# The order of a pair's seven products, and the steps of the work beside them, in an adaptive-norm block with linear attention and a Mish layer

## The chip, the cores and the metric

The kernel runs on one core of one Trainium2 chip. Its metric is the device time of one execution in microseconds, the median of several. A core has five engines with a queue of instructions each: TensorE (PE in the profile, its weight loads PEld), VectorE (DVE), ScalarE (ACT), GpSimd (POOL) and SyncE (SP, which here only starts DMAs).

## The reference

One sequence of 2048 tokens of width 512 goes through a block with two halves. Every product is in float32.

```
mod = silu(c) @ w_mod                       # six rows of 512: sa, ca, ga, sb, cb, gb
h = layernorm(x) * (1 + ca) + sa
x = x + ga * linear_attention(h) @ wo       # 32 heads of 16
h = layernorm(x) * (1 + cb) + sb
x = x + gb * (mish(h @ w1 + b1) @ w2)       # w1: 512 x 1792, w2: 1792 x 512
```

The change lies in the last line alone, in the product `h @ w1` with its Mish.

## The kernel before

**Tiles.** The tokens are worked on in four blocks of 512. The hidden width of 1792 is 14 columns of 128, and these go in 7 **pairs** (`g`). A tile is 128 partitions by 512. A float32 product is made of three products of halves: each operand is split into a high and a low half (`split`, L71: the high half by ScalarE at L75, the low half by VectorE at L80), and `mm3` or `product` multiplies high by high, low by high and high by low.

**Seven products for eight.** For two token blocks and two columns at once, the first layer is a 2 by 2 matrix product, and the kernel makes it with seven block products in place of eight (a scheme after Strassen and Winograd). A product (`product`, L911 to L919) is six matmuls of 128x512 at L917 into one PSUM bank. `pair_unit` (L933) issues the seven products of a pair:

- `a11*b11` by `pair_begin` (L924): written into a bank, the accumulator **p11**, and copied out by ScalarE as `u1` (L927),
- `s2*t2`, `s3*t3`, `s1*t1` and `a22*t4`, which VectorE adds up one after the other (`add`, L922: `u2`, `u3`, `c22`, again `u3`),
- `a12*b21`, which is added onto p11 (`pair_first`, L930), so that p11 is **written twice**, with ScalarE's copy between the writings,
- `s4*b22`, which is added onto the bank of `s1*t1`; VectorE then makes `c12` of it.

Four Mish evaluations follow on ScalarE: of `c22` and `c12` at once by `mish_b` (L909, for the other token block), and of p11 and the last `u3` by `mish` (L886, with its split, for this token block). That of p11 reads the PSUM bank itself.

**Banks.** PSUM has eight banks of one tile each, in three groups (`PBUFS`, L36): "acc" has 4, "h" has 3, "tp" has 1. A new tile of a group waits until the readers of the bank that it takes over are done. p11 takes the "tp" bank (in one pair of the last blocks an "acc" bank), the other products "h" banks.

**Order.** The order of the work is written out by hand: every engine gets its instructions in the order in which the program issues them, and works them in that order. Work beside the products is written as generators: `spawn` adds one to a list, and `tick` (L53) lets each generator on the list issue its next step. `pair_unit` has three ticks, and one tick follows every step of the second layer (`d_unit`, L891, in `trail`, L1003). On the list are, among others: `rows` (L575), which makes the operands of a later pair from w1 (four small sums on VectorE at L586 to L589, then splits); `w2_job` (L507), which scales two rows of w2 (L513), splits them and stores them; and `norm_tile` (L751), which normalizes one tile of 128 tokens for the blocks 2 and 3 in three steps: two sums on ScalarE (L210, L211); a small VectorE step (L215) and a power on GpSimd (L189); a small VectorE step (L219), the normalization on ScalarE (L198) and a store on GpSimd's DMA queue. Eight such tiles are taken from the list `tiles` in `trail`.

**Where the pairs stand.** For token blocks 0 and 1 there are seven pairs, from about 204 us on, with steps of the second layer of block 0 between them (twelve matmuls each; one step after each of the first two pairs, two steps later on). Pairs 0 and 1 have had both writings of p11 done ahead of the loop, so inside `pair_unit` p11 is written in pairs 2 to 6. Then follows the second layer of block 1 (`second`, L960). For blocks 2 and 3 ("the last blocks", `L` in the code) there are seven pairs in the order 5, 6, 0, 1, 2, 3, 4, from 357 us on; after all but the first of these `e_unit` (L1057) issues 24 narrow matmuls of the second layer, which is done by seven products as well, with `left_trail` (L1075) preparing its operands. From about 442 us on only the second layer is left.

Of the kernel before, what the change touches and what calls it, by code (L numbers as in the profile page):

```python
# [25 lines left out]
def block_kernel(ctx: ExitStack, tc: tile.TileContext, x, wqkv, wo, w1, b1t, w2, c, wmodt, out):  # L26
# [11 lines left out]
    def sb(name, dt=F32, shape=(P, 512)):  # L38

        return big.tile(list(shape), dt, tag="T", name=name, bufs=SLOTS)  # L40

    def ps(tag, name, shape=(P, 512)):
        return psp.tile(list(shape), F32, tag=tag, name=name, bufs=PBUFS[tag])
# [6 lines left out]
    def spawn(gen):  # L50
        fresh.append(gen)

    def tick():  # L53

        running.extend(fresh)
        fresh.clear()
        for g in list(running):
            if next(g, "end") == "end":
                running.remove(g)

    def run(gen):
        for _ in gen:
            pass
# [7 lines left out]
    def split(name, t, keep, key, lo_engine=dve, hi_engine=act):  # L71

        hi, lo = sb(f"{name}h", F32R, t.shape), sb(f"{name}l", F32R, t.shape)
        if hi_engine is act:
            act.activation(hi, t, AF.Copy)  # L75
        else:
            hi_engine.tensor_copy(hi, t)
        if lo_engine is dve:
            yield
        lo_engine.tensor_tensor(lo, t, f32(hi), op=ALU.subtract)  # L80
        keep[key] = hi, lo
# [18 lines left out]
    c0 = sb("c0")  # L100
# [474 lines left out]
    def rows(g, wait):  # L575

        r = [sb(f"w1p_{g}_{i}", F32, (P, 4, P)) for i in range(2)]
        for i in range(2):
            f = 2 * g + i
            sp.dma_start(r[i], w1[:, P * f:P * (f + 1)].rearrange("(k p) f -> p k f", p=P))  # L580
        for _ in range(wait):
            yield
        a11, a12, a21, a22 = [r[i][:, 2 * k:2 * k + 2, :] for i in range(2) for k in range(2)]
        s12, s34 = [sb(f"s{n}_{g}", F32, (P, 4, P)) for n in (12, 34)]
        s1, s2, s3, s4 = s12[:, 0:2, :], s12[:, 2:4, :], s34[:, 0:2, :], s34[:, 2:4, :]
        dve.tensor_tensor(s1, a21, a22, op=ALU.add)  # L586
        dve.tensor_tensor(s2, s1, a11, op=ALU.subtract)
        dve.tensor_tensor(s3, a11, a21, op=ALU.subtract)
        dve.tensor_tensor(s4, a12, s2, op=ALU.subtract)  # L589
        yield  # L590
        keep, todo = {}, []
        op_rows[g] = keep
        for name, v, parts in (("a1", r[0], ("a11", "a12")), ("s12", s12, ("s1", "s2")), ("s34", s34, ("s3", "s4")),
                               ("a22", a22, ("a22",))):
            half = split(f"{name}_{g}", v, keep, name)
            next(half)
            todo.append((name, half, parts))
            if len(todo) == 2:
                yield
                for name, half, parts in todo:  # L600
                    run(half)
                    for i, part in enumerate(parts):
                        op_a[g, part] = [h[:, 2 * i:2 * i + 2, :] for h in keep[name]]
                todo = []
# [3 lines left out]
    def store_rows(g):  # L608
        for name, halves in op_rows.pop(g).items():
            for i, h in enumerate(halves):  # L610
                rows_d[g, name, i] = drp.tile(list(h.shape), F32, name=f"rd_{g}_{name}_{i}")
                sp.dma_start(rows_d[g, name, i], f32(h))
# [138 lines left out]
    def norm_tile(b, t):  # L751

        v = xt.pop(("r", b, t))
        sums = act_sums("n", b, t, v)
        yield
        sums_eps("n", b, t, sums)
        yield
        sums_shift("n", b, t, sums)
        ln_apply("n", b, t, v, v, act)
        yield  # L760
        d = nd[b, t] = drp.tile([P, D], F32, name=f"nd_{b}_{t}")
        pool.dma_start(d, v)

    def load_back(key, src, b, t):
        v = xt[key, b, t] = sb(f"{key}b_{b}_{t}")
        sp.dma_start(v, src.pop((b, t)))
# [91 lines left out]
    for b in range(1, NB):  # L858
        for t in range(4):
            n = 4 * b + t  # L860
# [23 lines left out]
    def mish(p, b, f):  # L884
        u = ua[f] = sb(f"u_{b}_{f}")
        act.activation(u, p, AF.Mish, bias=b1c[:, f:f + 1])  # L886
        yield from split(f"a_{b}_{f}", u, ag, (b, f))
# [3 lines left out]
    def d_unit(b, f, n):  # L891
        if n == 0:
            for t in range(4):
                oacc[t] = ps("acc", f"oacc_{b}_{t}")
        for t in range(4):
            ts = slice(P * t, P * (t + 1))
            mm3(oacc[t], [a[:, ts] for a in ag[b, f]], w2s[f], n == 0, n == NF - 1)
            if n == NF - 1:
                v = xt["r", b, t]
                r0 = 512 * b + P * t  # L900
                dve.tensor_tensor(v, oacc[t], v, op=ALU.add)
                sp.dma_start(out[r0:r0 + P, :], v)
# [3 lines left out]
    def mish_b(p, f):  # L906

        u = ub[f] = sb(f"ub_{f}")
        act.activation(u, p, AF.Mish, bias=b1c[:, f:f + 1])  # L909

    def product(g, left, right, tag="h", onto=None):  # L911

        p = onto if onto is not None else ps(tag, f"p_{left}_{g}")
        for c in range(2):
            a, b = [h[:, c, :] for h in op_a[g, left]], op_b[right, c]
            for i, (st, mv) in enumerate(((a[0], b[0]), (a[0], b[1]), (a[1], b[0]))):
                pe.matmul(p, st, mv, start=onto is None and c == 0 and i == 0, stop=c == 1 and i == 2,  # L917
                          skip_group_check=onto is not None)
        return p  # L919

    def add(out, p, u):
        dve.tensor_tensor(out, p, u, op=ALU.add)  # L922

    def pair_begin(g, tag):  # L924

        u1, p = sb(f"u1_{g}"), product(g, "a11", "b11", tag)
        act.activation(u1, p, AF.Copy)  # L927
        return u1, p

    def pair_first(c0, g, p):  # L930
        spawn(mish(product(g, "a12", "b21", onto=p), c0, 2 * g))

    def pair_unit(c0, g, u1=None, tag="tp"):  # L933

        f = 2 * g
        u2, u3, c12, c22 = [sb(f"{n}_{g}") for n in ("u2", "u3", "c12", "c22")]
        p11 = None
        if u1 is None:
            u1, p11 = pair_begin(g, tag)
        add(u2, product(g, "s2", "t2"), u1)  # L940
        add(u3, product(g, "s3", "t3"), u2)
        tick()
        p = product(g, "s1", "t1")
        add(c22, p, u3)
        mish_b(c22, f + 1)
        add(u3, product(g, "a22", "t4"), u3)
        spawn(mish(u3, c0, f + 1))
        tick()
        if p11 is not None:
            pair_first(c0, g, p11)  # L950
        add(c12, product(g, "s4", "b22", onto=p), u2)
        mish_b(c12, f)
        tick()
# [14 lines left out]
    def ahead(b, u):  # L968

        if 0 <= u - NF + 4 < NF and last_first[u - NF + 4] < 2 * KEPT:  # L970
            w2_again(last_first[u - NF + 4])
        if 0 <= u - NF + 3 < NF:
            spawn(prep_a(b, last_first[u - NF + 3]))
# [27 lines left out]
        tick()  # L1001
    tiles = [norm_tile(b, t) for b in (2, 3) for t in range(4)]
    def trail(f):  # L1003
        if tiles:
            spawn(tiles.pop(0))
        d_unit(0, f, f)
        ahead(1, f)
        tick()

    for g in range(G + 1):  # L1010
        if g < G:
            for f in (2 * g, 2 * g + 1) if g else ():
                spawn(w2_job(f))
            if g == 0:
                spawn(rows(2, 3))
            pair_unit(0, g, begun[g][0] if g < 2 else None)
            if g < G - 2:
                store_rows(g)
            if 0 < g < G - 2:
                spawn(rows(g + 2, 2))  # L1020
            if g == G - 1:
                for n in range(8):
                    load_back("n", nd, 2 + n // 4, n % 4)
        for f in ((0,), (1,))[g] if g < 2 else (2 * g - 2, 2 * g - 1):
            trail(f)
# [4 lines left out]
    L = NB - 2  # L1030
# [44 lines left out]
    def left_trail(g):  # L1075
        yield
        yield
        yield from left_sums(g)
# [48 lines left out]
    for n, g in enumerate(pairs):  # L1127
        if n < 5:
            if n:
                load_rows(n)  # L1130
            if n:
                load_wb(pairs[n + 1])
        if n == 5:
            load_wb(pairs[6])
            load_r(0, 0)
        if n == 6:
            for m in pairs[:5]:
                load_wt("m4", m)
        pair_unit(L, g, tag="acc" if n == 1 else "tp")
        if n < EARLY:  # L1140
            spawn(left_trail(g))
        if n:
            e_unit(n - 1)
            tick()
# [69 lines left out]
```

## Time and profile before

| | |
|---|---|
| three runs | 500.35 us median (500.18 to 500.94) |
| the profiled execution | 500.48 us |
| its span, first to last instruction | 498.8 us |
| TensorE clock granted | 1.00 |
| ScalarE, VectorE busy | 264.5 us, 378.1 us |
| the matmuls of the pairs (L917), share of the chain that ended last | 15% `p_s`, 11% `p_a` |

The profile takes one execution. Its page gives each engine's busy time, the chain of work that ended last, and the costliest groups of instructions. A row of a timeline is: start and duration in microseconds, engine, line, operation, output and inputs, shapes, how many instructions it stands for, and in brackets how long the engine was idle before it and what ended that. Names lose their numbers: `p_a` is a bank of `a11`, `a12` or `a22`, `p_s` one of `s1` to `s4`; `c` is `c12` or `c22`, and `ub` the Mish of it; `u` is `u1`, `u2`, `u3` or the Mish of p11 or `u3`, told apart by line and input. In the list of waits a row names the waiting group, what ended the wait, the total, the count and the longest.

### The profile page before, as it was taken

What the parts mean: (1) busy time and instruction counts of PE and PEld (TensorE: products, weight loads), DVE (VectorE), ACT (ScalarE), POOL (GpSimd) and SP (SyncE); (2) the same over time, 40 slices, a digit from 0 to 9 for tenths busy, and PEclk for the clock granted to TensorE, in tenths of its full rate; (3) what the DMA queues carried; (4) which work ended last, traced back from release to release, by engine and by line L of the source; (5) the groups of instructions that cost most, each with busy time, mean ns of one, the idle gap of its engine ahead of it and who ended that gap; (6) DMA issues with size and microseconds to landing.
All of it is one profiled execution on the core that took longest, in us unless ns stands there. A gap on an engine that the chain in (4) does not pass through costs nothing.

```text
span 498.8 us, 7659 instructions
## 1 busy us (share of the span) xinstructions
PE 491.2 (98%) x2648; PEld 412.7 (83%) x2648; DVE 378.1 (76%) x730; ACT 264.5 (53%) x472; POOL 137.3 (28%) x238
## 2 busy tenths in 40 slices
PE   7999999999999999999999999999999999999997
PEld 6778888878778888888878888888888888899997
DVE  6889875889997979976876865689875666669671
ACT  6776674533351889736577765187243444469000
POOL 3571000100212324100343323323463231444300
PEclk9999999999999999999999999999999999999999
DMA  8821413381454307397799594999997273789412
GB/s 298 293 84 44 152 37 106 126 277 43 131 149 130 94 19 261 124 372 236 227 360 347 196 309 147 314 345 359 377 368 203 63 191 85 181 201 257 103 43 85
DMA packets 65613, 96.49 MB, mean 193 GB/s; under 512 B 7277, under 2 KB 31733, under 8 KB 65574
## 3 DMA queue, kind: packets, MB, share of 16 engines
q1 hardware_dynamic: 37220, 52.51, 31.7%
q0 software_dynamic: 28208, 43.21, 30.7%
q8 instruction: 21, 0.34, 0.3%
q10 hardware_dynamic: 146, 0.26, 0.1%
q14 instruction: 18, 0.15, 0.1%
HBM read 62.92 MB, written 33.03 MB: 192 GB/s over the span
## 4 chain that ended last, share of the span: by engine, by line
PE 93%; DVE 3%; ACT 2%; DMA 1%; issue 1%; POOL 0%; ACTq 0%
PE p_s L917 15%; PE p_a L917 11%; PE oacc L69 5%; PE oacc L67 5%; PE oacc L68 5%; PE m L67 5%; PE m L69 5%; PE m L68 5%; PE o L67 3%; PE pq L67 3%; PE o L69 3%; PE o L68 3%; PE pq L69 3%; PE pq L68 3%; PE gacc L68 3%; PE gacc L69 3%
## 5 line engine op out<-in xcount | busy, mean ns | idle before, releaser
L909 ACT ACTIVATE ub<-c,b1c 128x512 f32<-128x512 f32 x28 | 20.1, 719 | 57.5 <-DVE c L922 57.5
L922 DVE TENSOR_TENSOR c<-p_s,u 128x512 f32<-128x512 f32 x28 | 19.3, 689 | 24.1 <-PE p_s L917 24.0
L922 DVE TENSOR_TENSOR u<-p_s,u 128x512 f32<-128x512 f32 x28 | 19.4, 692 | 22.7 <-PE p_s L917 12.7
L189 POOL TENSOR_TENSOR rs_n<-rs_n,half 128x1 f32<-128x1 f32 x16 | 9.8, 615 | 55.1 <-DVE rs_n L215 45.5
L1125 POOL DMA_DIRECT2D wt_m<-w2t x20 | 14.0, 704 | 24.6 <-PE p_a L917 11.0
L241 ACT ACTIVATE e_q<-pq 128x512 f32<-128x512 f32 x16 | 9.4, 590 | 19.9 <-PE pq L69 19.9
L775 ACT ACTIVATE hf_n<-tp_n,mc 128x512 f32<-128x512 f32 x16 | 11.7, 770 | 14.9 <-PE tp_n L773 14.9
L241 ACT ACTIVATE e_k<-pk 128x512 f32<-128x512 f32 x16 | 9.4, 591 | 13.2 <-PE pk L69 12.9
L189 POOL TENSOR_TENSOR rs_x<-rs_x,half 128x1 f32<-128x1 f32 (+1 forms) x10 | 7.1, 718 | 32.2 <-DVE rs_x L184 31.4
L573 POOL DMA_DIRECT2D w2b<-w2d x20 | 10.7, 541 | 18.0 <-DMA out_dram<-r 5.6
L927 ACT ACTIVATE u<-p_a 128x512 f32<-128x512 f32 x14 | 8.3, 591 | 13.6 <-PE p_a L917 12.1
L243 DVE TENSOR_SCALAR e_k<-e_k 128x512 f32<-128x512 f32 x16 | 7.1, 444 | 9.8 <-ACT e_k L241 9.7
L681 POOL DMA_DIRECT2D rden_d<-rden x3 | 2.2, 741 | 43.4 <-DVE rden L679 43.4
L198 ACT ACTIVATE x<-x,nb_x,rs_x 128x512 f32<-128x512 f32 x15 | 11.6, 807 | 4.6 <-DVE nb_x L193 3.5
L922 DVE TENSOR_TENSOR u<-p_a,u 128x512 f32<-128x512 f32 x14 | 9.7, 692 | 5.7 <-PE p_a L917 5.0
L567 POOL DMA_DIRECT2D wb<-w2d x14 | 9.9, 711 | 12.1 <-PE p_a L917 9.3
L693 DVE TENSOR_TENSOR q<-q,rd 128x512 f32<-128x512 f32 x16 | 10.5, 687 | 3.6 <-DMA rd<-rden_d 3.5
L198 ACT ACTIVATE r<-r,nb_n,rs_n 128x512 f32<-128x512 f32 x8 | 6.5, 812 | 12.0 <-DVE nb_n L219 9.2
L244 DVE SCALAR_TENSOR_TENSOR ku<-pk,e_k 128x512 f32<-128x512 f32 x16 | 11.1, 692 | 0.7
L244 DVE SCALAR_TENSOR_TENSOR q<-pq,e_q 128x512 f32<-128x512 f32 x16 | 11.1, 692 | 0.7
L705 DVE TENSOR_TENSOR r<-o,r 128x512 f32<-128x512 f32 x16 | 10.9, 679 | 0.9 <-PE o L69 0.7
L886 ACT ACTIVATE u<-u,b1c 128x512 f32<-128x512 f32 x14 | 10.0, 715 | 2.6 <-DVE u L922 2.2
(1328 smaller groups left out, 1924.7 us busy)
## 6 DMA issues: line engine op xcount, KB each, us to landing
wm<-in_wmodt_dram SPq DMA_DIRECT2D x24, 256.0 KB, 5.1
w2b<-w2d POOLq DMA_DIRECT2D x20, 256.0 KB, 6.7
wt_m<-w2t POOLq DMA_DIRECT2D x20, 256.0 KB, 3.8
r<-in_x_dram SPq DMA_DIRECT2D x16, 256.0 KB, 2.6
x<-in_x_dram SPq DMA_DIRECT2D x15, 256.0 KB, 4.7
w1p<-in_w_dram SPq DMA_DIRECT2D x14, 256.0 KB, 3.8
w2r<-in_w_dram SPq DMA_DIRECT2D x14, 256.0 KB, 3.0
wb<-w2d POOLq DMA_DIRECT2D x14, 256.0 KB, 4.8
```

The costliest lines, as they stand in the source:

```text
L67: pe.matmul(o, st[0], mv[0], start=start, stop=False)
L68: pe.matmul(o, st[0], mv[1], start=False, stop=False)
L69: pe.matmul(o, st[1], mv[0], start=False, stop=stop)
L189: pool.tensor_tensor(y, y, half[:, lo:hi], op=ALU.pow)
L198: act.activation(dst, t, AF.Identity, bias=nb[key, b][:, j:j + 1], scale=rs[key, b][:, j:j + 1])
L241: act.activation(e, p, AF.Exp)
L244: dve.scalar_tensor_tensor(dst, p, 0.0, e, op0=ALU.max, op1=ALU.add)
L775: act.activation(hf[b, j], p, AF.Identity, bias=mc[:, 12 + j:13 + j], scale=mc[:, 16 + j:17 + j])
L909: act.activation(u, p, AF.Mish, bias=b1c[:, f:f + 1])
L917: pe.matmul(p, st, mv, start=onto is None and c == 0 and i == 0, stop=c == 1 and i == 2, skip_group_check=onto is not None)
L922: dve.tensor_tensor(out, p, u, op=ALU.add)
L1125: pool.dma_start(v, w2t[g][:, :, SUM[name], :])
```

## The change

`pair_unit` issues the products in another order, with other banks and other steps for the ticks:

| place | before | after |
|---|---|---|
| P1 | `a11*b11` in "tp" | `a11*b11` in "tp" |
| P2 | `s2*t2` in "h" | `s2*t2` in "h", then tick |
| P3 | `s3*t3` in "h", then tick | `a12*b21` onto p11 |
| P4 | `s1*t1` in "h" | `s3*t3` in "h" |
| P5 | `a22*t4` in "h", then tick | `s1*t1` in "h", then tick |
| P6 | `a12*b21` onto p11 | `a22*t4` in "tp" |
| P7 | `s4*b22` onto `s1*t1`, then tick | `s4*b22` onto `s1*t1`, then tick |

So one product, not four, stands between the two writings of p11; the Mish of p11 is issued by the second tick of the pair, not by the third; and `a22*t4` takes over the bank of p11. The second pair of the last blocks has p11 in "tp" like the others, no longer in "acc". Of the eight token tiles, one starts before each of the pairs 1 to 4 and the others in `trail`, at its first step and at every odd one, where before each step of `trail` took one.

```diff
-    def pair_unit(c0, g, u1=None, tag="tp"):
+    def pair_unit(c0, g, u1=None):
...
-            u1, p11 = pair_begin(g, tag)
+            u1, p11 = pair_begin(g, "tp")
         add(u2, product(g, "s2", "t2"), u1)
+        tick()
+        if p11 is not None:
+            pair_first(c0, g, p11)
         add(u3, product(g, "s3", "t3"), u2)
-        tick()
         p = product(g, "s1", "t1")
         add(c22, p, u3)
         mish_b(c22, f + 1)
-        add(u3, product(g, "a22", "t4"), u3)
+        tick()
+        add(u3, product(g, "a22", "t4", "tp"), u3)
         spawn(mish(u3, c0, f + 1))
-        tick()
-        if p11 is not None:
-            pair_first(c0, g, p11)
         add(c12, product(g, "s4", "b22", onto=p), u2)
         mish_b(c12, f)
         tick()
...
     def trail(f):
-        if tiles:
+        if tiles and (f == 0 or f % 2):
             spawn(tiles.pop(0))
...
                 spawn(rows(2, 3))
+            if g and tiles:
+                spawn(tiles.pop(0))
             pair_unit(0, g, begun[g][0] if g < 2 else None)
...
-        pair_unit(L, g, tag="acc" if n == 1 else "tp")
+        pair_unit(L, g)
```

## The prediction, made before the changed kernel ran

> **What bounds the kernel now.** I read the page first: busy shares, then the chain that ended last, then the list of who waited for whom, and after that the timeline of each engine around the pairs.
>
> ```profile
> span 498.8 us, 7659 instructions
> ...
> PE 491.2 (98%) x2648; PEld 412.7 (83%) x2648; DVE 378.1 (76%) x730; ACT 264.5 (53%) x472; POOL 137.3 (28%) x238
> ```
>
> ```profile
> PE m L67 <- ACT u L886: 0.5, 1, 0.5
> ```
>
> TensorE is busy 98% of the span, so every microsecond in which it must wait is added to the end, and there is hardly a wait that an edit could take away. The second fence is the only wait that the wait list shows for TensorE behind the first stage; it will be of use below. The question is thus not what the change saves, but whether it makes TensorE wait. ScalarE is busy only 53%, but that is no protection: what counts is how long the chain through its queue is, not how full it is.
>
> The rows from which all prices come: first TensorE, then VectorE, then ScalarE, each in order of time (start, duration, engine, line).
>
> ```profile
> 233.85 0.39 PE L917 MATMUL p_a<-b_0h,a_2h 128*128 128x512 f32 x1
> ...
> 235.21 0.39 PE L917 MATMUL p_s<-t_0h,s_2h 128*128 128x512 f32 x1
> ...
> 375.96 0.39 PE L917 MATMUL p_s<-b_1h,s_6l 128*128 128x512 f32 x1
> ...
> 378.22 0.28 PE L69 MATMUL m<-wb,a_11l 128*128 128x256 f32 x1
> 378.98 0.39 PE L67 MATMUL m<-wb,a_11h 128*128 128x256 f32 x1 [0.48 <-ACT u L886]
> 379.21 0.28 PE L68 MATMUL m<-wb,a_11h 128*128 128x256 f32 x1
> ```
>
> ```profile
> 232.45 0.68 DVE L80 TENSOR_TENSOR s_2l<-s,s_2h 128x512 fp32r<-128x512 f32 x1
> ...
> 234.59 0.69 DVE L80 TENSOR_TENSOR a_3l<-u,a_3h 128x512 fp32r<-128x512 f32 x1
> ...
> 241.20 0.69 DVE L922 TENSOR_TENSOR u<-p_a,u 128x512 f32<-128x512 f32 x1
> 241.81 0.42 DVE L586 TENSOR_TENSOR s<-w1p 128x256 f32<-128x256 f32 x1
> ...
> 243.27 0.15 DVE L219 TENSOR_TENSOR nb_n<-sums_n,rs_n 128x1 f32<-128x1 f32 x1
> ...
> 376.39 0.69 DVE L922 TENSOR_TENSOR c<-p_s,u 128x512 f32<-128x512 f32 x1 [2.03 <-PE p_s L917]
> ```
>
> ```profile
> 243.51 0.82 ACT L198 ACTIVATE r<-r,nb_n,rs_n 128x512 f32<-128x512 f32 x1 [1.65 <-DMA w2d<-w_2h]
> 244.23 0.71 ACT L886 ACTIVATE u<-u,b1c 128x512 f32<-128x512 f32 x1
> 244.97 0.63 ACT L75 ACTIVATE a_5h<-u 128x512 fp32r<-128x512 f32 x1
> 245.51 0.71 ACT L909 ACTIVATE ub<-c,b1c 128x512 f32<-128x512 f32 x1
> ...
> 248.92 0.40 ACT L75 ACTIVATE a_3h<-w1p 128x256 fp32r<-128x256 f32 x1
> 249.23 0.62 ACT L75 ACTIVATE w_4h<-w2r 128x512 fp32r<-128x512 f32 x1
> ...
> 251.73 0.62 ACT L210 ACTIVATE scrap_n<-r 128x512 f32<-128x512 f32 x1
> ...
> 253.19 0.58 ACT L927 ACTIVATE u<-p_a 128x512 f32<-128x512 f32 x1
> ...
> 377.12 0.72 ACT L909 ACTIVATE ub<-c,b1c 128x512 f32<-128x512 f32 x1 [1.33 <-DVE c L922]
> 377.75 0.61 ACT L75 ACTIVATE l_5h<-ub 128x512 fp32r<-128x512 f32 x1
> 378.27 0.67 ACT L886 ACTIVATE u<-p_a,b1c 128x512 f32<-128x512 f32 x1
> ```
>
> Read from them: a product of six matmuls takes 1.36 us (233.85 to 235.21), a matmul of it 0.23. VectorE begins to add a product 0.43 after its last matmul began (375.96 to 376.39). The Mish of the sum begins 0.73 later (376.39 to 377.12), the next ScalarE instruction 0.63 after that, and each further split 0.52. The Mish of an accumulator takes 0.67. A normalization (L198) holds ScalarE for 0.72 (243.51 to 244.23), a Mish with its own split for 0.74 and 0.54, the half-wide split for 0.31, two w2 splits and the two sums of one token tile for 2.50 (249.23 to 251.73), of which one tile is 1.46 (251.73 to 253.19, a tile of the same length).
>
> TensorE's one wait shows what a held accumulator costs. The Mish of p11 ran from 378.27 to 378.94, the matmul that needed its bank began 0.04 later, and the next one 0.23 after that, where narrow matmuls otherwise follow each other by 0.12. So a restart costs 0.04 and then 0.11.
>
> **The change part by part.** Call the seven products of a pair P1 to P7 in the order in which they are issued. In 12 pairs (2 to 6 of block 0, all seven of the last blocks) p11 is written inside the pair, in the single "tp" bank. Before, P6 was its second writing and a22*t4 stood at P5 in an "h" bank. Afterwards P3 is the second writing and a22*t4 is P6, **in that same "tp" bank**: it may not start until ScalarE's Mish has read p11. That Mish is issued only by the second tick of the pair, behind the Mish of c22, which waits for P5 and two additions on VectorE. As ScalarE works its queue in order, P6 waits for a chain that begins at P5's end. The order of the built program's instructions agrees: P6's first matmul waits for ScalarE's L886 of p11, in all 12 pairs.
>
> *The new wait before P6.* From P5's last matmul: 0.43 to the addition of c22, 0.73 to its Mish, 0.63 to the next place in the queue, 0.67 for the Mish of p11, 0.04 and 0.11 for the restart, less the 0.23 at which P6 would have followed: 2.38. For 12 pairs 28.6. Other work stands between the two Mishes in some pairs, by the program's order on ScalarE: two splits (1.04) in pair 5 of block 0 and the first of the last blocks; one split (0.52) in four later pairs there; two splits and a normalization (1.76) in pairs 3 and 4; in pair 2 a normalization that itself waits for VectorE. There the four sums of the next rows follow c22: 0.61 for the addition (241.20 to 241.81), 1.46 for the sums (to 243.27), 0.24 until the normalization began (243.51), then its 0.72: 3.03 instead of 1.36, or 1.67 more. Together 2.08 + 2.08 + 3.52 + 1.67 = 9.35. This part: 37.9. Behind P6 on TensorE stand P7 and the second layer's products; they start late by as much and catch nothing up, since TensorE has no slack.
>
> *One product between the writings.* ScalarE must copy p11 (L927, 0.58) while P2 runs. In the later pairs it is idle by then. In four pairs it isn't, counted from the order of its queue. Pair 2: c12's addition begins 0.43 after P7's last matmul, which twelve matmuls separate from P1 at 233.85, so at 231.33; 0.61 for it, 2.14 for two splits and the two scalings of w2 (232.45 to 234.59), 0.24 to the normalization at 234.32; then 0.72 + 0.74 + 0.54 to the w2 splits, 2.50 to the copy at 238.82, its end at 239.40. P3 could have begun at 236.57; it waits 2.87 + 0.11 = 3.0. The same count from P6's start gives 0.5 in pairs 3 and 4, where ScalarE has one normalization and one tile in front of the copy, and 0.8 in the second pair of the last blocks, which follows with no second-layer work between. Sum 4.8.
>
> *What it saves.* Three "h" products a pair in three banks no longer collide, and the second pair of the last blocks leaves the "acc" banks, so the wait at 378.98 goes: 0.76 less 0.12, and the 0.11, so 0.75. Nothing else on TensorE can be saved that the wait list names.
>
> *The token tiles and moved ticks.* Eight tiles are normalized in both. One by one they start before the pairs 1 to 4 and at odd steps of the second layer, and the last is stored before pair 5 instead of in it, while it is loaded back only at pair 6; its GpSimd power and store, and SP's loads of w1 and w2 rows, keep their order in their queues. I cost this at nothing beyond what is counted above: a store or load that comes somewhat late is hidden by the 2.4 to 4 us in which TensorE now waits in every pair; were that cover gone, it would cost what it is late.
>
> Sum: 37.9 + 4.8 - 0.75 = 41.95 on the profiled execution of 500.48 (span 498.8 and 1.7 around it): 542.4. The runs' median is 0.13 lower, so **542.3**. The bounds: were none of the work between the two Mishes in the way, 9.35 less, 533; the other end is in the rivals.
>
> **The rivals.**
>
> *The clock drops.* Waits of 3.7 to 3.9 us idle time arise in pairs 2 to 4 (2.38 + 1.7, with the restart and the last matmul's own 0.39 taken off and 0.23 put back). What the trace shows of such idleness is its last stretch:
>
> ```profile
> 495.00:498.80 3.80, 0.34 (x3) 0.14 (x2) 0.42 (x1) 0.00 (x0) 0.00 (x0) 1.00 0.10 35
> ```
>
> TensorE idle for 3.46 us, granted clock still 1.00. Three waits here are longer than that. If each cost as much again at half clock as the idle time lasted, 3.8 us of work done in 7.6, the loss would be 3.8 each: 11; with half as long a slow stretch, 6: 548. The Trainium skill, "TensorE: Matmul & The Clock Gate", section "Why this matters for your kernels", says that a TensorE idle for more than about 3 us falls back to half clock; by that all of the longest five waits would, and the time would be above this rival's 548. The last stretch of the trace does not show such a fall within 3.46 us. 15%.
>
> *P5's sum is late.* Four pairs (3 to 5, and the first of the last blocks, which has those of a w2 pair) have four small sums on VectorE, 1.46 as above, between the addition of P2 and that of P4. The new order leaves them the time of P3 and P4, 2.7, and I count them as hidden. Were they late by their whole length, c22 and so the Mish of p11 would come 4 x 1.46 = 5.8 later: 548. 10%.
>
> *Little between the Mishes.* If the splits are done before c22's Mish can start, only 2.38 x 12 remains: 533. Against it: a queue worked in order. 8%.
>
> *P6 finds its bank free.* If the wait before P6 is covered (the new bank is another), only the copies count: 500.35 + 4.8 - 0.75 = 504.4. 3%.
>
> *The other side: faster.* Two writings so close free p11 early, and the bank could be empty when P6 comes. For that the Mish of p11 must begin 0.7 us before P5 ends, so it must stand ahead of c22's Mish in the queue; the whole price depends on that one order. With it, and with copies in time, the gain is the 0.75: 499.6. The program's order speaks against it. 3%, a third of it so small a gain that it would count as none.
>
> **How the numbers follow.** Forecast 61%, 542.3, by its own errors (0.15 us a wait) 539 to 545. The range 532 to 549 takes in the three rivals at 533 and 548 and leaves out 504, 499 and the worst of the clock. About 0.2% is what a measurement of this kernel can tell from no change. Slower 97%, faster 2% and same 1% (the last rival).
>
> **What would show each step.** In the new profile's wait list, TensorE's L917 waits for ScalarE's L886 12 times, some 36 us in all, 2.2 to 4 each; for L927 four times, the longest near 3 in pair 2. In the chain that ended last ScalarE and VectorE gain most of the 40 us that TensorE loses in share. The stretches without pairs keep their length. Wrong would be: waits on L886 that are shorter than 2 us; TensorE's clock below 1.00 in the middle; a copy that no one waits for.

## The result, and the profile after

The changed kernel takes 556.95 us (median of four runs, 556.69 to 560.61), the kernel before 500.5 in the four runs beside it: the ratio is 1.114, with a 95% interval of 1.110 to 1.119. That is slower, as forecast, but by 56 us where 42 were forecast, and outside the range of 532 to 549. The profiled execution took 556.94 us.

The page of the changed kernel: its span, the busy times, and the row of TensorE's granted clock in 40 slices.

```profile
span 555.2 us, 7655 instructions
...
PE 510.7 (92%) x2648; PEld 423.2 (76%) x2648; DVE 377.7 (68%) x730; ACT 264.5 (48%) x472; POOL 136.8 (25%) x238
...
PEclk9999999999999999988897999999898989889999
```

VectorE and ScalarE are busy for as long as before. TensorE has the same 2648 matmuls and is busy for 510.7 us in place of 491.2. Waits explain little of that. Waiting is not busy time, and only the two ends of a wait add to it, 0.27 us each time as worked out below: 4.3 us for 16 waits, of the 19.5. The last row says where the rest comes from: in the slices of the pairs the granted clock is below full speed, which it was nowhere before. The same row of the kernel before:

```profile
PEclk9999999999999999999999999999999999999999
```

The list of waits of the changed kernel (engine, line, what ended the wait; total, count, longest):

```profile
PE p_a L917 <- ACT u L886: 34.7, 12, 3.9
PE p_a L917 <- ACT u L927: 3.7, 4, 2.7
```

These are the waits that the prediction asked for, in number, total and length. The list is of idle time. A stall is 0.27 longer than that: the matmul before it is listed as 0.39 long where the next would follow after 0.23, and the first matmul behind it takes 0.11 more (so the prediction's 2.38 stands beside 2.11 in the rows below). With this it is 34.7 + 3.7 + 16 x 0.27 = 42.7 us, and 37.9 + 4.8 was forecast.

One plain pair (6 of block 0) in the timeline of the changed kernel, from P5's last matmul to P6:

```profile
327.13 0.39 PE L917 MATMUL p_s<-t_1h,s_6l 128*128 128x512 f32 x1
327.56 0.69 DVE L922 TENSOR_TENSOR c<-p_s,u 128x512 f32<-128x512 f32 x1 [0.67 <-PE p_s L917]
328.28 0.72 ACT L909 ACTIVATE ub<-c,b1c 128x512 f32<-128x512 f32 x1 [5.57 <-DVE c L922]
328.91 0.67 ACT L886 ACTIVATE u<-p_a,b1c 128x512 f32<-128x512 f32 x1
...
329.63 0.50 PE L917 MATMUL p_a<-t_0h,a_6h 128*128 128x512 f32 x1 [2.11 <-ACT u L886]
```

It is the forecast's chain, step for step: 0.43 to the addition, 0.72 to the Mish of c22, 0.63 to the next place in ScalarE's queue, 0.67 for the Mish of p11, 0.05 to P6. P6 would have begun at 327.36; it begins 2.27 later and its second matmul 0.11 later still: 2.38.

So the waits are explained, and 14.6 us are not. They are in the clock. The trace records when it changes: from 200 us to the end of the span it is at half speed in ten windows of 3.413 us, all of them on one grid of that step. Cut on this grid, some of the changed kernel's windows look like this (busy time and count for each engine in turn, TensorE's first; then the granted clock):

```profile
core 0: us, PE busy (x) PEld busy (x) DVE busy (x) ACT busy (x) POOL busy (x), PEclk, DMA share, GB/s
...
235.68:239.09 3.41, 0.70 (x4) 0.28 (x3) 0.86 (x2) 3.38 (x9) 0.00 (x0) 1.00 0.73 223
239.09:242.50 3.41, 3.41 (x9) 2.64 (x10) 1.79 (x4) 1.23 (x4) 1.53 (x3) 0.50 0.02 5
...
327.84:331.25 3.41, 1.62 (x7) 1.36 (x8) 0.41 (x1) 1.93 (x3) 0.00 (x0) 1.00 0.33 103
331.25:334.66 3.41, 3.41 (x17) 2.83 (x16) 2.67 (x5) 1.25 (x2) 0.00 (x0) 1.00 0.00 0
406.34:409.76 3.42, 1.62 (x8) 1.00 (x6) 1.38 (x2) 1.03 (x2) 0.00 (x0) 1.00 0.02 4
409.76:413.17 3.41, 3.10 (x14) 2.56 (x15) 0.69 (x2) 0.89 (x2) 0.00 (x0) 1.00 0.00 0
488.26:491.68 3.42, 1.31 (x6) 0.75 (x6) 0.74 (x2) 1.93 (x3) 0.84 (x2) 1.00 1.20 289
491.68:495.09 3.41, 3.41 (x10) 2.63 (x9) 0.69 (x1) 0.00 (x0) 1.40 (x2) 0.50 0.43 109
```

They are read in twos: what a window held, and what the clock was in the next one. A window with 0.70 us of work, or 1.31, is followed by half clock; windows with 1.62 are not. In a full window at full clock some 16 or 17 matmuls are listed, at half clock 9 or 10: each such window loses 7 matmuls of 0.227, or 1.6 us, and ten are 16 at most. The wait that lies in the window from 488.26 on is no longer than that of pair 6 above, which no half clock follows:

```profile
491.05 0.50 PE L917 MATMUL p_a<-t_0h,a22b 128*128 128x512 f32 x1 [2.11 <-ACT u L886]
```

The theory from here on: **the waits cost what was forecast, and the rest is the clock, which is cut for a window when TensorE worked for less than about half of the window before.** Rivals: the rest is in waits, restarts or late sums that the list doesn't show; or it is the clock, but by the length of a single idle time. Beside this stands what sets the 42.7: the bank of p11, the place of its Mish in the queue, the tiles.

### The profile page after: what moved, and what is told of

The parts are those of the page before. It is cut to its first block, busy times and chain, and to the rows that moved or that the text cites. A ratio compares the mean times of both kernels' runs of the same rounds, so it can differ in the third digit from the quotient of the medians.

```text
span 555.2 us, 7655 instructions
## 1 busy us (share of the span) xinstructions
PE 510.7 (92%) x2648; PEld 423.2 (76%) x2648; DVE 377.7 (68%) x730; ACT 264.5 (48%) x472; POOL 136.8 (25%) x238
## 4 chain that ended last, share of the span: by engine, by line
PE 84%; ACT 6%; DVE 4%; DMA 3%; issue 2%; POOL 0%; SPq 0%; ACTq 0%
PE p_s L917 13%; PE p_a L917 11%; PE m L67 4%; PE m L68 4%; PE m L69 4%; PE oacc L69 4%; PE oacc L67 4%; PE oacc L68 4%; PE o L67 3%; PE pq L67 3%; PE o L69 3%; PE o L68 3%; PE pq L69 3%; PE pq L68 3%; PE gacc L68 2%; PE gacc L69 2%
## 5 line engine op out<-in xcount | busy, mean ns | idle before, releaser
L922 DVE TENSOR_TENSOR u<-p_a,u 128x512 f32<-128x512 f32 x14 | 9.7, 691 | 51.4 <-PE p_a L917 51.4
L922 DVE TENSOR_TENSOR u<-p_s,u 128x512 f32<-128x512 f32 x28 | 19.3, 691 | 31.9 <-PE p_s L917 26.1
L922 DVE TENSOR_TENSOR c<-p_s,u 128x512 f32<-128x512 f32 x28 | 19.4, 692 | 24.1 <-PE p_s L917 23.9
L917 PE MATMUL p_a<-t_0h,a22b 128*128 128x512 f32 x10 | 5.2, 518 | 12.6 <-ACT u L886 12.6
L927 ACT ACTIVATE u<-p_a 128x512 f32<-128x512 f32 x14 | 8.3, 592 | 14.6 <-PE p_a L917 14.6
L567 POOL DMA_DIRECT2D wb<-w2d x14 | 9.9, 709 | 19.5 <-PE p_a L917 13.1
L917 PEld LDWEIGHTS p_a<-t_0h,a22b 128*128 128x128 f32 x10 | 2.1, 211 | 15.0 <-ACT u L886 14.7
L620 POOL DMA_DIRECT2D a1b<-rd_a x10 | 5.4, 541 | 30.9 <-DVE u L922 13.2
L762 POOL DMA_DIRECT2D nd<-r x8 | 4.5, 565 | 34.2 <-ACT r L198 34.2
```

## The experiments

Seven more kernels ran, and the changed one a second time, each beside the kernel before (medians of 500.36 and 500.32 us).

### Work added that no one reads

```diff
+    def fill(g, n):
+        p = ps("h", f"fill_{g}")
+        for _ in range(n):
+            pe.matmul(p, op_a[g, "s2"][0][:, 0, :], op_b["t2", 0][0], start=True, stop=True)
...
+        if c0 == 0 and g == 2:
+            fill(g, 11)
         if p11 is not None:
             pair_first(c0, g, p11)
...
+        if p11 is not None:
+            fill(g, 15 if c0 == 0 and g < 5 else 9)
         add(u3, product(g, "a22", "t4", "tp"), u3)
```

> The changed kernel with work added that no one reads: matmuls into a free "h" bank ahead of P6 (9 in a pair, 2.0 us; 15 in the pairs 2 to 4 of block 0, 3.4 us) and ahead of P3 of pair 2 (11, 2.5 us). They fit into the waits, so that the waits' ends do not move. Theory, the 14.6 us above the forecast are the clock, which falls after a stretch in which TensorE did too little: granted clock 1.00 in all windows, the matmuls take 0.23 us each throughout, time 541 to 544 although 150 matmuls are added. Rival, the 14.6 us are waits, restarts or late sums that the wait list doesn't count: time stays at 556 to 558, or rises by the added work (150 x 0.227 = 34 us) if the waits aren't there to hold it.

Measured: **541.99 us** (541.79 to 542.82), 15.0 less than the changed kernel, with 137 matmuls more (the count by the edit; the 150 of the expectation was a slip). Its page and its waits:

```profile
span 540.3 us, 7933 instructions
...
PE 526.5 (97%) x2785; PEld 437.7 (81%) x2785; DVE 377.9 (70%) x730; ACT 264.7 (49%) x472; POOL 137.4 (25%) x238
...
PEclk9999999999999999999999999999999999999999
```

```profile
PE p_a L917 <- ACT u L886: 6.0, 9, 1.2
PE p_a L917 <- ACT u L932: 1.2, 4, 0.6
```

The added work fills the waits, and the clock stays at full speed until the last matmul has ended. The waits themselves are still there, only filled (L932 is L927, five lines down). So 542.0 is the time of the changed kernel without the clock's part, and the forecast for that was 542.3. Doing more made it faster: the 15.0 us were the clock. The rival of uncounted waits falls.

### The changed kernel once more

No edit: the same kernel, profiled again.

> The changed kernel once more, for a second profile. Its waits of TensorE are the same in every execution to 0.1 us; the grid of 3.41 us on which the clock changes need not begin at the same place. Theory, the share of a window: another set of waits is followed by half clock than in the first profile, namely those for which one window of the grid holds less than about 1.55 us of work, so a wait of 2.1 us may be followed by half clock that wasn't and the other way round; the number of such windows is 8 to 13 and the time goes with it by 1.5 us a window. Rival, the length of the idle time: the same waits as in the first profile, the longest above all.

Measured: 560.70 us. The waits for the Mish of p11 in this second profile, and two of them in its timeline:

```profile
PE p_a L917 <- ACT u L886: 34.7, 12, 3.9
```

```profile
311.18 0.50 PE L917 MATMUL p_a<-t_0h,a_5h 128*128 128x512 f32 x1 [3.15 <-ACT u L886]
...
410.68 0.67 PE L917 MATMUL p_a<-t_0h,a_6h 128*128 128x512 f32 x1 [2.11 <-ACT u L886]
```

The same twelve waits, to the tenth (those for the copy add up to 3.5 us, 3.7 in the first profile). But the grid begins elsewhere, and now twelve windows are at half clock, among them those from 311.86 and 410.85 on, behind these two waits. In the first profile nothing followed them:

```profile
312.26 0.50 PE L917 MATMUL p_a<-t_0h,a_5h 128*128 128x512 f32 x1 [3.15 <-ACT u L886]
...
410.07 0.50 PE L917 MATMUL p_a<-t_0h,a_6h 128*128 128x512 f32 x1 [2.11 <-ACT u L886]
```

The windows around the second of them, in the second profile:

```profile
407.43:410.85 3.42, 1.31 (x7) 0.77 (x6) 1.20 (x2) 1.49 (x3) 0.00 (x0) 1.00 0.02 3
410.85:414.26 3.41, 3.41 (x9) 2.67 (x10) 0.69 (x1) 0.44 (x1) 0.00 (x0) 0.50 0.00 0
```

The wait of 2.11 us lies wholly in one window here (1.31 us of work); in the first profile the window ended, at 409.76, before the wait did, and held 1.62. Same wait, same length, other price: the length of an idle time alone doesn't decide. Against the 541.99 of the filled kernel, twelve windows cost 18.7 us and the ten of the first profile 15.0: 1.5 to 1.6 each. That is also why the runs of this kernel spread over 4 us where those of the kernel before spread over 1: the run of 560.61 us has a mean granted clock of 0.962, like this second profile, and the other three have 0.969.

### Each wait cut in two

```diff
         tick()
+        product(g, "s4", "b22", onto=p, part=range(1))
         add(u3, product(g, "a22", "t4", "tp"), u3)
         spawn(mish(u3, c0, f + 1))
-        add(c12, product(g, "s4", "b22", onto=p), u2)
+        add(c12, product(g, "s4", "b22", onto=p, part=range(1, 6)), u2)
```

> The changed kernel with the first of P7's six matmuls issued ahead of P6, where it waits only for the addition of c22: each wait is cut in two (some 0.9 and 1.1 us in the plain pairs, 0.9 and 1.6 with one split, 0.9 and 2.8 in the pairs 2 to 4), the total is as before but for that one matmul, 0.23 a pair. What it tells apart is the cause of the falls of the clock. Theory, the share of a window of 3.41 us in which TensorE works: windows that held 0.8 to 1.5 us of work hold 0.23 more, so in the last blocks one to four half-clock windows are left out of five, although no idle time there but the first exceeds 1.7 us; in the pairs 2 to 4 all stay; in all 546 to 553. Rival, the length of one idle time, above 2.1 us: no half-clock window behind 400 us, those of the pairs 2 to 4 stay; 544 to 547.

Measured: 555.86 us (555.15 to 557.51), ten windows at half clock. Its waits, the two of one pair in its timeline, and two windows of the last blocks with those that follow (L919 is L917, L924 is L922):

```profile
PE p_a L919 <- ACT u L886: 19.2, 12, 2.6
PE p_s L919 <- DVE c L924: 11.0, 14, 0.8
```

```profile
407.74 0.50 PE L919 MATMUL p_s<-b_0h,s_6h 128*128 128x512 f32 x1 [0.78 <-DVE c L924]
409.06 0.50 PE L919 MATMUL p_a<-t_0h,a_6h 128*128 128x512 f32 x1 [0.83 <-ACT u L886]
```

```profile
406.24:409.65 3.41, 1.80 (x8) 0.93 (x7) 0.78 (x2) 1.90 (x3) 0.00 (x0) 1.00 0.00 0
409.65:413.07 3.42, 3.42 (x10) 2.68 (x9) 0.69 (x1) 0.03 (x1) 0.00 (x0) 0.50 0.00 0
488.16:491.57 3.41, 1.80 (x7) 1.05 (x6) 0.69 (x1) 1.93 (x3) 0.43 (x1) 1.00 1.15 276
491.57:494.99 3.42, 3.42 (x11) 2.75 (x10) 0.89 (x2) 0.00 (x0) 1.76 (x3) 0.50 0.49 119
```

In the first window of each two TensorE was never idle for longer than 0.83 us, and the clock fell in the second. The rival by length expected no half clock behind 400 us; there are five such windows. So that rival falls. The theory's own numbers missed too: it expected 546 to 553 us and up to four windows at half clock in the last blocks, and there are six. Busy time misled: each burst of matmuls ends with a modelled tail of some 0.16 us (0.39 long, 0.23 to the next), and a window with two gaps holds one tail more. The count does not have that tail. Over the three profiles, between 200 and 500 us, of the full-clock windows with fewer than ten matmuls, those with six or fewer were all followed by half clock (25 of 25), with seven five of eight, with eight one of nine, with nine none of two. A window has room for 15 (3.413 / 0.227), and the counts include those that reach over its edges; so the border lies somewhat below half. Also, two waits more than planned came in, in pairs 0 and 1 (14 on L924, not 12), 2.1 us.

The border can be read closer. Count each wide matmul as 0.227 us of work (a narrow one as 0.12), with its end 0.15 us before the listed one, for the tail; the 0.15 is chosen, and anything from 0.05 to 0.25 separates the windows too. Then, in the seven profiles of the changed kernel and its variants, between 200 and 500 us, the 35 full-clock windows that were followed by half clock held at most 1.36 us of work each, and the other 536 held at least 1.47. So the border lies near two fifths of a window, at about six wide matmuls of the 15.

### a22*t4 in an "h" bank again

```diff
-        add(u3, product(g, "a22", "t4", "tp"), u3)
+        add(u3, product(g, "a22", "t4"), u3)
```

> The changed kernel with one edit: a22*t4 (P6) goes into an "h" bank again, all else as changed. Theory, the bank sets the price: P6 no longer waits for the Mish of p11, so the twelve waits on L886 (34.7 us idle, some 38 with the restarts) and the half-clock windows that they cause (some 15 us) go together; the four waits on the copy L927 stay (2.7, 0.2, 0.2, 0.6 idle, 4.8 with the restarts); the collisions of the "h" banks stay gone (0.75 and a few tenths). Time 500.4 + 4.8 - 1.6 = 503.6, and up to 2 more if the wait in pair 2 falls into one window of the clock: 503 to 506. Rival, the moved ticks and the other order cost by themselves (sums late on VectorE, ScalarE's queue in another order) and the bank is only where it shows: waits appear elsewhere, time above 520.

Measured: **506.07 us** (504.5 to 506.2), ratio 1.011 with an interval of 1.009 to 1.012; one window at half clock, behind the wait of pair 2.

```profile
PE p_a L917 <- ACT u L927: 3.9, 3, 2.7
...
PE p_a L917 <- ACT u L886: 0.5, 1, 0.5
```

One word of the change takes back 51 of its 56 us. The twelve waits are gone; the 0.5 left is another, P1 of the second pair of the last blocks, which follows so closely that the Mish of p11 of the pair before still has the "tp" bank. The rest adds up: four waits of 4.4 us idle and 0.27 more each, 5.5; less the 0.75 saved; one window, 1.5: 6.3, and 5.8 were measured in the profiled execution. The time came out just above the expected 503 to 506, as the window came in and the copy of pair 3 is now waited for by 0.97 us, not 0.2. My reading of the latter is that in the changed kernel the wait of P6 gave ScalarE time to catch up; no run tests that. One of the four runs, 504.5 us, has a mean granted clock of 1.000 where the others (506.03 to 506.2) have 0.997: the price of one window once more, 1.6.

### The Mish of p11 ahead of c22's in the queue

```diff
         p = product(g, "s1", "t1")
+        tick()
         add(c22, p, u3)
         mish_b(c22, f + 1)
-        tick()
         add(u3, product(g, "a22", "t4", "tp"), u3)
```

> The changed kernel with one edit: the second tick of a pair is issued ahead of the addition and the Mish of c22, so that the Mish of p11 stands ahead of c22's in ScalarE's queue; a22*t4 stays in the bank of p11. Theory, the place in the queue sets the price: the Mish of p11 ends long before P5 does, the twelve waits on L886 vanish or shrink to at most 1 us in the pairs 2 to 4 (there sums, splits, a normalization and the Mish are 3.9 us on ScalarE in the 4.1 us of P3 to P5); the waits on the copy L927 stay at 4.8. Time 504, range 501 to 507. Rival, reusing the bank within a pair is too early whatever the order of the queue: waits of 2 us and more stay in most pairs, time above 530.

Measured: 511.86 us (510.28 to 514.21); the profiled execution, 514.21, has three windows at half clock, all in pair 2.

```profile
PE p_a L917 <- ACT u L886: 4.5, 4, 2.0
PE p_a L917 <- ACT u L927: 3.7, 4, 2.7
```

With the bank still shared, the place in the queue alone takes eight of the twelve waits away and 45 us. So it takes both to make the price: the second use of the bank in the same pair, and the Mish behind c22's. The rival, that most waits would stay at 2 us and more, falls. But the time is 5 above the range. The expectation had the waits on L886 too low: four stay, of 1.98 us in pair 2, 0.91 in pairs 3 and 4, and 0.74 in the first pair of the last blocks, for which none was expected. With 0.27 each they cost 5.6, the copies 4.8, and 0.75 is saved: 510.0. The two fastest runs, with a mean granted clock of 0.999, took 510.28 and 510.68. The rest is the clock again: three windows at 1.4 each bring the profiled execution to 514.21. In pair 2 the normalization ahead of the Mish of p11 waits for its own input until 247.45. The row of it on ScalarE:

```profile
247.45 0.81 ACT L198 ACTIVATE r<-r,nb_n,rs_n 128x512 f32<-128x512 f32 x1 [6.38 <-DVE nb_n L219]
```

### The tiles alone, and the order alone

The first has the kernel before with the third part of the change alone, the tiles one by one; the second has the kernel that came to 506.07, with the tiles as before.

```diff
-        if tiles:
+        if tiles and (f == 0 or f % 2):
             spawn(tiles.pop(0))
...
+            if g and tiles:
+                spawn(tiles.pop(0))
             pair_unit(0, g, begun[g][0] if g < 2 else None)
```

> The kernel before with the third part of the change alone: the token tiles one by one, from before pair 1 on and at odd steps of the second layer. Theory, the tiles cost TensorE nothing in the old order, as ScalarE's copy and Mish have four products' time there: no new wait on L927 or L886, 499.8 to 500.8. Rival, the later tiles put ScalarE's queue behind by themselves and are what makes the copies late: waits on L927 of 0.5 to 3 us in the pairs 2 to 4, 502 to 505.

Measured: 500.44 us (eleven runs), ratio 1.0001 with an interval of 0.9992 to 1.001. The tiles cost nothing in the old order. One wait on L886 is new, for P1 of pair 3, where none was expected; it is 0.2 us long, and the time doesn't show it.

```diff
-        if tiles and (f == 0 or f % 2):
+        if tiles:
             spawn(tiles.pop(0))
...
-            if g and tiles:
-                spawn(tiles.pop(0))
```

> The kernel with a22*t4 in "h" (the experiment above that came to 506.07) with the token tiles as before: the order of the products and the moved ticks alone. Theory, the copies are late because P3 follows P1 by one product, whatever the tiles do: three or four waits on L927 stay, in pair 2 between 1.2 (by where the copy ended in the trace of before) and 3, 502.5 to 506. Rival, the one-by-one tiles put the sums and normalizations in front of the copies: without them the waits on L927 go, 499.8 to 501.

Measured: 506.26 us (504.71 to 506.29), the same as with the tiles one by one.

```profile
PE p_a L917 <- ACT u L927: 3.8, 4, 1.8
```

The waits for the copy come with either order of the tiles, only at other pairs: 0.36 us in pair 2, 1.78 in pair 3 and 0.81 in pairs 4 and 5, in place of 2.71, 0.97 and 0.21 in pairs 2 to 4. So the rival falls, but the expectation of 1.2 to 3 us in pair 2 missed, and 506.26 lies just above its range; one window at half clock, behind the wait of pair 3, is in it. It is the new order, with its ticks, that brings the waits: one product, 1.36 us, is too little cover for a copy that stands in ScalarE's queue. No run moves the ticks without the order.

### The second writing one product earlier, not three

```diff
         p = product(g, "s1", "t1")
+        if p11 is not None:
+            pair_first(c0, g, p11)
         add(c22, p, u3)
...
-        if p11 is not None:
-            pair_first(c0, g, p11)
         add(c12, product(g, "s4", "b22", onto=p), u2)
...
-        pair_unit(L, g, tag="acc" if n == 1 else "tp")
+        pair_unit(L, g)
```

> A version meant to beat both: the kernel before, with the second writing of p11 moved up by one product (from P6 to P5, so three products stand between the writings), a22*t4 as P6 in its "h" bank, tiles as before, and the second pair of the last blocks in "tp". The Mish of p11 is then issued by the second tick, behind that of c22, but nothing in the pair waits for its bank. Theory: it ends some 2.5 us after P4, P5 to P7 last 4.1, so the "tp" bank is empty when the next pair begins, and the 0.48 us wait for an "acc" bank with its restart goes: 0.75 less, 499.6 (499.3 to 500.0). Rival, the Mish of p11 comes too late for the next pair's P1, or the splits behind it delay the Mish of c12: a new wait of 0.5 us and no gain, 500.2 to 501.5.

Measured: 501.58 us (eleven runs), ratio 1.0022 with an interval of 1.0013 to 1.0031: slower than the kernel before by little. There are two new waits in the timeline. The second is the one that the rival named, P1 of the next pair waiting for the Mish of p11; the first, P7 of pair 3 waiting for the addition of c22, neither side expected:

```profile
258.26 0.50 PE L917 MATMUL p_s<-b_2h,s_3h 128*128 128x512 f32 x1 [0.67 <-DVE c L922]
...
368.38 0.50 PE L917 MATMUL p_a<-b_0h,a_6h 128*128 128x512 f32 x1 [0.77 <-ACT u L886]
```

They cost 0.67 + 0.77 + 2 x 0.27 = 2.0, less the 0.75 saved: 1.2, and 1.26 were measured. The second of them shows where my 2.5 us went wrong (ScalarE, before it):

```profile
365.99 0.73 ACT L909 ACTIVATE ub<-c,b1c 128x512 f32<-128x512 f32 x1 [6.18 <-DVE c L922]
366.62 1.14 ACT L75 ACTIVATE t_4h<-t 128x512 fp32r<-128x512 f32 x2
367.66 0.67 ACT L886 ACTIVATE u<-p_a,b1c 128x512 f32<-128x512 f32 x1
```

The work that the tick issues stands in VectorE's queue ahead of the addition of c22, which begins at 365.21, 2.3 us after P4's last matmul (362.87) and not 0.43; and its two splits stand ahead of the Mish of p11. No version here beats the kernel before.

## Why the prediction was wrong, by its steps

- **The wait before P6: right.** Twelve waits with the chain, its order and its durations as worked out; 37.9 forecast, 34.7 + 12 x 0.27 = 37.9 found. Also the work between the two Mishes: 2.63 us idle with one split, 3.15 and 3.25 with two, 3.74 to 3.85 in pairs 2 to 4.
- **The copies: right.** 4.8 forecast, 3.7 + 4 x 0.27 = 4.8 found, with pair 2 the longest (2.71 idle). **The tiles: right**, 500.44 us with them alone, beside 500.36.
- **What is hidden, and what it saves: right** to a few tenths, as 541.99 for the filled kernel shows, against 542.3.
- **The clock: wrong, and it is the step that failed.** The prediction had it as a rival with 15%, for the three waits that are "longer than that", 3.46 us, at 548. In the sum that gave 542.3 it stood at nothing. The ground for that was the row of the last stretch, "TensorE idle for 3.46 us, granted clock still 1.00". That row could not tell: it ended at 498.8, and the clock does not answer within a window, but in the next. The trace of before does record a fall, at 499.97, past the end of what that row shows and behind a window without a matmul (the two rows below). The unit of the price was wrong as well, in the rival too. It isn't the few longest waits that count: each of the thirteen of 2.1 us and more is a draw, by the phase of the grid and the work around it. Ten windows were lost (twelve in the other profile), 1.5 us each: 15.0 us, as the filled kernel shows, in place of nothing in the sum and of three losses of two to four in the rival.

```profile
496.55:499.97 3.42, 0.00 (x0) 0.00 (x0) 0.00 (x0) 0.00 (x0) 0.00 (x0) 1.00 0.11 38
499.97:500.78 0.81, 0.00 (x0) 0.00 (x0) 0.00 (x0) 0.00 (x0) 0.00 (x0) 0.50 0.00 0
```

- **The rivals on the waits**: neither the late sum of P5 nor the wait without splits came; all twelve have the length worked out with the work that stands in each.
- **The chain that ended last: half right.** ScalarE and VectorE gain five points of the nine that TensorE loses; DMA and issue have gained the rest. Before, then after:

```profile
PE 93%; DVE 3%; ACT 2%; DMA 1%; issue 1%; POOL 0%; ACTq 0%
```

```profile
PE 84%; ACT 6%; DVE 4%; DMA 3%; issue 2%; POOL 0%; SPq 0%; ACTq 0%
```

- "TensorE's clock below 1.00 in the middle" was named among what would prove the forecast wrong, and did.

The Trainium skill, "TensorE: Matmul & The Clock Gate", section "Part 1: The HAM clock gate", has the window as 3413 ns and free-running; the traces agree, with a step of 3.413 us and another phase in each profile. The same page of the Trainium skill, section "Why this matters for your kernels", asks for no idle gaps above some 3 us between bursts of matmuls. By that rule the prediction counted five waits. The runs differ: two gaps of 0.78 and 0.83 us in one window were enough (the fall at 409.65 in the kernel with the wait cut in two), and one of 3.15 us that lay across two windows was not (312.26 in the first profile).

What stays open: where between 1.36 and 1.47 us the border lies, as the ends of matmuls are modelled; and whether weight loads count as work. No run separates these.

## What to carry to other kernels

A bank that is used twice within a step makes its second user wait for all that stands in the emptying engine's queue up to the read that frees the bank. Worked out in order, that queue gave the waits here to a tenth of a microsecond. Then cost the waits twice: once as idle time, and once for the clock: here 1.5 us for every window of 3.4 us in which TensorE works for less than about two fifths, however the idle time in it is cut up. If a wait can't be removed, filling it with matmuls that no one reads gave back 15 of 56 us here.

## What the runs showed of the hardware

- The granted clock fell to half for one whole window of 3.413 us behind each window with six or fewer wide matmuls (25 of 25), and as a rule came back in the next. Twice it stayed down for two, behind a half-clock window that was itself not full: from 290.29 in the first profile, with six matmuls, and from 239.00 in the kernel with the Mish of p11 ahead, with seven. All other half-clock windows list eight or more, and full speed followed. So the border, counted in matmuls, seems to be about the same at either clock.

```profile
286.88:290.29 3.41, 0.30 (x2) 0.00 (x0) 0.82 (x3) 2.34 (x4) 0.55 (x1) 1.00 0.58 202
290.29:293.70 3.41, 2.66 (x6) 2.15 (x7) 0.00 (x0) 1.32 (x3) 0.59 (x1) 0.50 0.52 154
293.70:297.12 3.42, 3.42 (x9) 2.64 (x8) 1.25 (x2) 0.00 (x0) 0.00 (x0) 0.50 0.00 0
```

- The list of waits and the share of busy time both hide such a loss: matmuls at half clock count as busy (510.7 us in place of 491.2, 15.2 of it not from the ends of the waits). The row of the clock shows it, and the spread of the runs (4 us in place of 1) hints at it.
